# Retention and two MLPs on one core: a batch's last two units in one transfer, whole units further ahead, position factors grown on ScalarE

## The chip, the cores and the metric

The kernel runs on one core of a Trainium2 chip. The metric is the device time of one execution in microseconds, the median over several runs. It is compared with the same time of the changed kernel; lower is better.

## The reference

What is computed is a retention layer (attention without softmax, with a decay in place of it) and two MLPs behind it, all in float32:

```python
scores = scale * np.matmul(q, k.transpose(0, 1, 3, 2))          # 4 batches, 8 heads, 576 positions, 64
gamma = 1.0 - 2.0 ** (-5.0 - np.arange(H))
Dmat = np.where(rel >= 0, gamma[:, None, None] ** rel[None, :, :], 0.0)   # rel = i - j
x = np.matmul(scores * Dmat, v)                                 # as 2304 tokens x 512
h = x @ w_in                                                    # 512 x 2048
x = (h * np.tanh(softplus(h))) @ w_out                          # Mish
h = x @ w2_in
out = (h * sigmoid(1.702 * h)) @ w2_out                         # 2304 x 512
```

## The kernel before

A *unit* is one batch's chunk of 128 positions, all eight heads. A batch has five units; the last holds only 64 positions. So there are 20 units, 0 to 19, and units 4, 9, 14 and 19 are the short ones. The attention loop goes over the units in order. For each unit TensorE multiplies keys and queries (`sc`, line 772), adds to a running sum of keys times values (`ds`, line 795, in PSUM; a copy of it, `state`, is made by ScalarE), and multiplies out (`o`, lines 823 and 834): the state with the queries, then the masked scores `pm` with the values. VectorE makes `pm` from `sc` (line 776) and writes X, which is `o` times position factors `gt` (line 848). GpSimd multiplies the values by the decay (line 761). The scores of unit u + 1 stand on TensorE ahead of unit u's update and outputs.

The position factors `gt` of the first chunk are grown from 16 columns to 128 by doubling, on VectorE (lines 854 and 856); those of the later chunks come from the first by ScalarE. The tables for this ride behind unit 0's data, in the same buffer.

All loads are issued by SP, in the order in which the program writes them, to one DMA queue of 16 engines. A whole unit is one transfer of 1 MB (queries, keys twice, values; rows of 8 KB). A short unit is two transfers, of 128 x 2 KB and 64 x 2 KB. There are five unit buffers, used in turn, and a unit's load is written four units ahead of its use (`UNITS_AHEAD`): a load into a used buffer waits on SP until TensorE and GpSimd are done with the unit that was in it, and everything behind it on SP waits too. The first two weights of the first MLP (`w1[0]`, `w1[1]`, 1 MB each) are fetched between the units at the places that `EARLY_AT` gives; the other weights follow behind the last unit. They are converted in several steps on VectorE, ScalarE and GpSimd in the gaps of the attention loop. Their places in SBUF (`w0` to `w9` of the pool `keep`) are empty until then.

The first MLP's blocks begin on TensorE inside the last three units of the attention loop; behind these come the layers, about 750 us long, in which TensorE is the busy engine.

Of the kernel before, what the change touches and what calls it, by code (L numbers as in the profile page):

```python
# [8 lines left out]
F32 = mybir.dt.float32  # L9
# [5 lines left out]
ALU = mybir.AluOpType  # L15
# [3 lines left out]
B, H, S, D = 4, 8, 576, 64  # L19
NT, DM, DFF = 2304, 512, 2048  # L20
P = 128
NPAIR = H // 2
# [3 lines left out]
CH = [(c, min(P, S - c)) for c in range(0, S, P)]  # L26
NCH = len(CH)
UNITS = [(b, c) for b in range(B) for c in range(NCH)]
# [31 lines left out]

KEPT = 10
X_UNITS = (4, 5, 6, 7, 10, 11, 12, 13)
EARLY_AT = ((1, 5), (7, 13))
EARLY = len(EARLY_AT)
LATE = [-2 + 1.95 * i for i in range(NM - EARLY)]
UNITS_AHEAD = 4
GROW = (16, 32, 64)
TABLES = NCH * H + NPAIR * (NCH + len(GROW) + GROW[0])
FIRST = 4 * DM + (TABLES + 15) // 16 * 16

# [23 lines left out]


@with_exitstack
def retention_mish_gelu_kernel(ctx: ExitStack, tc: tile.TileContext, qkv, w1, w2, first_unit, out):
    nc = tc.nc  # L100
    keep = ctx.enter_context(tc.tile_pool(name="keep", bufs=1))
    dram = ctx.enter_context(tc.tile_pool(name="dram", bufs=1, space=DRAM))
# [16 lines left out]
    def act(o, i, f=AF.Copy, scale=1.0, bias=0.0):  # L119
        nc.scalar.activation(out=o, in_=i, func=f, scale=scale, bias=bias)  # L120
# [18 lines left out]
    def plan(name, step, job):  # L139
        plans.setdefault(name, []).append((step, job))  # L140
        plans[name].sort(key=lambda p: p[0])

    def position(name, step):
        for j in [j for j in under_way if j[1] == name]:
            j[1] = next(j[0], None)
            if j[1] is None:
                under_way.remove(j)
        while plans.get(name) and plans[name][0][0] <= step:
            job = plans[name].pop(0)[1]
            then = next(job, None)  # L150
            if then:
                under_way.append([job, then])
# [8 lines left out]
    def fetch(m):  # L161

        raw = place(m + 1).tile([P, 2 * DM], I64, tag=f"w{m + 1}", name="raw")
        if m < EARLY:
            nc.sync.dma_start(out=raw, in_=w1[m])
        else:
            for i in range(2):
                nc.sync.dma_start(out=raw[:, i * DM : (i + 1) * DM], in_=w1[m][:, i * DM : (i + 1) * DM])
        held[m] = raw.rearrange("p (q n) -> p q n", q=4)
        return  # L170
        yield
# [122 lines left out]
    n_u = len(UNITS)  # L294
# [8 lines left out]

    for m, (loaded_in, converted_in) in enumerate(EARLY_AT):
        plan("fetch", loaded_in - n_u, fetch(m))
# [177 lines left out]
    while not units or sum(units[-1]) < N_ROUND * STEPS:  # L483
        first = sum(units[-1]) if units else 0
# [214 lines left out]
    def attention():  # L699
        with tc.tile_pool(name="att", bufs=1) as ap:  # L700
            loaded = {}

            def load(u):
                if u >= len(UNITS):
                    return
                b, c = UNITS[u]
                n = CH[c][1]
                t = buffers[u % len(buffers)]
                w = NPAIR * n
                if n < P:  # L710
                    pieces = [(P, 0, 2 * w), (n, 2 * w, 2 * w + DM)]
                else:
                    pieces = [(P, 0, 2 * DM), (P, 2 * DM, FIRST)] if u == 0 else [(P, 0, 4 * DM)]
                for rows, e0, e in pieces:
                    nc.sync.dma_start(out=t[:rows, e0:e], in_=first_unit[:, e0:e] if u == 0 else qkv[b, c, :rows, e0:e])
                loaded[u] = (
                    t[:, :w].rearrange("p (c s) -> p c s", c=NPAIR),
                    t[:, w : 2 * w].rearrange("p (c s) -> p c s", c=NPAIR),
                    t[:, 2 * w : 2 * w + DM],
                    t[:, 2 * w + DM : 2 * w + 2 * DM],  # L720
                )

            state = [ap.tile([P, NPAIR, P], F32, name=f"state{i}") for i in range(2)]
            for t in (state[1][:, 0], state[1][:, 1:]):
                nc.gpsimd.memset(t, 0.0)
            nc.vector.memset(state[0], 0.0)
            buffers = [
                ap.tile([P, 4 * DM if i else FIRST], F32, name=f"unit{i}") for i in range(UNITS_AHEAD + 1)
            ]
            tab = buffers[0][:, 4 * DM : 4 * DM + TABLES]  # L730
            vt = tab[:, : NCH * H].rearrange("p (c h) -> p c h", c=NCH)
            per_pair = tab[:, NCH * H :].rearrange("p (c n) -> p c n", c=NPAIR)
            steps, grow, first = (
                per_pair[:, :, :NCH],
                per_pair[:, :, NCH : NCH + len(GROW)],
                per_pair[:, :, NCH + len(GROW) :],
            )
# [4 lines left out]
                out=cm, in_=cm, pattern=[[1, P]], compare_op=ALU.is_ge, fill=0.0, base=0, channel_multiplier=-1  # L742
            )
            gt = ap.tile([P, NCH, NPAIR, P], F32, name="gt")
# [4 lines left out]

            act(column[:, :1], state[0][:, 0, :1], AF.Mish)  # L750

            load(1)
            for u in range(2, UNITS_AHEAD):
                load(u)
            pm, sums, now = {}, [None], [None]

            def decay_v(u):
                b, c = UNITS[u]
                n = CH[c][1]
                vv = loaded[u][2][:n].rearrange("p (h d) -> p h d", d=D)  # L760
                nc.gpsimd.tensor_tensor(  # L761
                    out=vv, in0=vv, in1=vt[:n, c, :].unsqueeze(2).to_broadcast([n, H, D]), op=ALU.mult
                )

            def scores(u):
                n = CH[UNITS[u][1]][1]
                qt, kt = loaded[u][:2]
                sc = [quarters(bank("sc", (0, 1, 2, 3))) for _ in range(2)]
                for p in range(NPAIR):
                    for j in range(2):  # L770
                        sl = slice(64 * j, 64 * j + 64)
                        nc.tensor.matmul(sc[j][:n, p, :n], lhsT=kt[sl, p, :], rhs=qt[sl, p, :], start=True, stop=True)  # L772
                pm[u] = []
                for j in range(2):
                    t = ap.tile([P, NPAIR, P], F32, tag="pm", name="pm", bufs=4)
                    nc.vector.tensor_tensor(  # L776
                        out=t[:n, :, :n],
                        in0=sc[j][:n, :, :n],
                        in1=cm[:n, :n].unsqueeze(1).to_broadcast([n, NPAIR, n]),
                        op=ALU.mult,  # L780
                    )
                    pm[u].append(t)
# [21 lines left out]
            def take(u):  # L804

                if UNITS[u][1] == NCH - 1:
                    return None
                for j in range(2):
                    sl = slice(64 * j, 64 * j + 64)
                    act(state[u % 2][sl, :, sl], sums[0][sl, :, :D])  # L810
                return state[u % 2]
# [39 lines left out]

            scores(0)
            decay_v(0)
            nc.vector.tensor_copy(out=gt[:, 0, :, : GROW[0]], in_=first)
            for j, w in enumerate(GROW):
                nc.vector.tensor_tensor(  # L856
                    out=gt[:, 0, :, w : 2 * w],
                    in0=gt[:, 0, :, :w],
                    in1=grow[:, :, j : j + 1].to_broadcast([P, NPAIR, w]),
                    op=ALU.mult,  # L860
                )
            for u in range(n_u):
                step = u - n_u
                load(u + UNITS_AHEAD)
                if u + 1 < n_u:
                    decay_v(u + 1)
                position("pool", step)
                position("fetch", step)
                if 1 < u < n_u - 1:
                    scores(u + 1)  # L870
                update(u)
                now[0], before = take(u), now[0]
                o = outputs(u, before)
                if u == 1:
                    scores(u + 1)
                if u < NCH - 1:
                    n = CH[u + 1][1]
                    for p in range(NPAIR):
                        act(gt[:, u + 1, p, :n], gt[:, 0, p, :n], scale=steps[:, p, u + 1 : u + 2])
                position("act early", step)  # L880

                if u == n_u - 2:
                    elementwise(0, jobs=False)
                finish(u, o)
                if u == n_u - 1:
                    elementwise(1, jobs=False)
                if u == 0:
                    scores(1)
                position("vector", step)
                position("act late", step)  # L890
                if u in X_UNITS:
                    k = X_UNITS.index(u)
                    split_x((0, SIDE)[k // NK], k % NK)()
                if u == n_u - 3:
                    up(0)
                if u == n_u - 2:
                    up(1)
# [101 lines left out]
```

## Time and profile before

| | |
|---|---|
| median of 3 runs | 819.74 us (818.33 to 820.0) |
| the profiled execution | 818.37 us |
| its span, first to last instruction | 816.6 us |
| TensorE (PE) busy | 810.1 us, 99% |
| VectorE (DVE) busy | 554.2 us, 68% |
| ScalarE (ACT) busy | 405.4 us, 50% |
| GpSimd (POOL) busy | 114.9 us, 14% |
| attention stage | from the start to about 72.7 us |

The span is what the profiler saw of the program; the time of the execution has 1.8 us around it. Busy TensorE is counted from pipelined matmuls, so 99% means that it hardly stood still, not that it ran at its peak. The attention stage is the only one that the change touches.

### The profile page before, as it was taken

How to read it: one execution, taken by the hardware profiler on the slowest of the kernel's cores; microseconds unless marked ns; L12 is line 12 of the kernel's file. 1: busy time of each engine (PE TensorE's matmuls, PEld its weight loads, DVE VectorE, ACT ScalarE, POOL GpSimd, SP SyncE). 2: the span in 40 equal slices, each digit the busy share in tenths (PEclk: the TensorE clock that was granted, in tenths of full speed). 3: DMA queues.
4: the chain of work that ended last, by engine and by line, in shares of the span. 5: the costliest groups of instructions: out<-in, count | busy, mean ns of one | idle time of the engine just before them, and what ended most of it. 6: DMA issues, size and time to landing. Idle time of an engine off the chain costs nothing.

```text
span 816.6 us, 13465 instructions
## 1 busy us (share of the span) xinstructions
PE 810.1 (99%) x5104; PEld 742.1 (91%) x5104; DVE 554.2 (68%) x1030; ACT 405.4 (50%) x748; POOL 114.9 (14%) x124
## 2 busy tenths in 40 slices
PE   9999999999999999999999999999999999999998
PEld 8898888888888888888888899999999999999998
DVE  4886866655876778777645455699655898555776
ACT  4445766664554556455443333566233665233553
POOL 3442322221122214133210000000000000000000
PEclk9999999999999999999999999999999999999999
DMA  9999600002487749578531377787877878877774
GB/s 348 381 342 406 259 1 0 1 10 94 149 243 220 238 128 271 169 233 246 178 102 41 110 272 254 240 275 253 321 254 235 269 271 265 297 255 244 261 266 168
DMA packets 96048, 175.01 MB, mean 214 GB/s; under 512 B 5232, under 2 KB 67184, under 8 KB 90224
## 3 DMA queue, kind: packets, MB, share of 16 engines
q1 hardware_dynamic: 95840, 173.96, 63.3%
q8 instruction: 40, 0.66, 0.3%
q14 instruction: 24, 0.20, 0.1%
q10 hardware_dynamic: 144, 0.20, 0.1%
HBM read 140.06 MB, written 34.08 MB: 213 GB/s over the span
## 4 chain that ended last, share of the span: by engine, by line
PE 96%; DMA 2%; DVE 1%; ACT 0%; POOL 0%; issue 0%; SPq 0%; DVEq 0%
PE h L348 24%; PE acc L369 24%; PE p L592 21%; PE p L637 21%; PE sc L772 2%; PE o L834 2%; DMA unit<-qkv_dram 1%; PE o L823 1%; PE ds L795 1%; DMA unit<-first_unit_dram 1%; DVE pm L776 0%; DVE gt L856 0%; POOL unit L761 0%; DVE X L848 0%; DVE g L398 0%
## 5 line engine op out<-in xcount | busy, mean ns | idle before, releaser
L369 PE MATMUL acc<-g,w 128*128 128x512 f32 (+1 forms) x960 | 209.5, 368 | 0.0
L369 PEld LDWEIGHTS acc<-g,w 128*128 128x128 f32 x960 | 168.4, 189 | 30.4
L348 PE MATMUL h<-x,w 128*128 128x512 f32 x768 | 184.7, 390 | 0.1
L592 PE MATMUL p<-xop,ring 128*128 128x384 f32 x1008 | 175.2, 334 | 0.0
L637 PE MATMUL p<-g,ring 128*128 128x384 f32 x1008 | 175.2, 334 | 0.0
L592 PEld LDWEIGHTS p<-xop,ring 128*128 128x128 f32 x1008 | 174.8, 188 | 0.1
L637 PEld LDWEIGHTS p<-g,ring 128*128 128x128 f32 x1008 | 174.8, 188 | 0.0
L348 PEld LDWEIGHTS h<-x,w 128*128 128x128 f32 x768 | 143.8, 188 | 30.4 <-DVE w L237 0.5
L398 DVE TENSOR_TENSOR g<-c,g 128x512 fp32r<-128x512 f32 x80 | 55.6, 695 | 103.4 <-ACT g L120 103.2
L120 ACT ACTIVATE g<-cs 128x384 fp32r<-128x384 f32 x168 | 87.8, 524 | 63.3 <-PE p L637 62.4
L430 DVE TENSOR_TENSOR g<-cs,g 128x384 fp32r<-128x384 f32 x168 | 92.5, 557 | 26.1 <-ACT g L120 25.0
L120 ACT ACTIVATE g<-c 128x512 fp32r<-128x512 f32 x80 | 47.2, 589 | 113.1 <-PE acc L369 112.4
L120 ACT ACTIVATE cs<-cs 128x384 f32<-128x384 f32 x72 | 37.8, 526 | 111.6 <-DVE cs L430 111.6
L200 POOL TENSOR_TENSOR cy<-cr 128x256 int32<-128x256 int32 x64 | 54.2, 866 | 178.2 <-DVE cr L196 94.5
L120 ACT ACTIVATE c<-h 128x512 f32<-128x512 f32 x80 | 44.2, 552 | 44.8 <-PE h L348 41.4
L430 DVE TENSOR_TENSOR cs<-cs 128x384 f32<-128x384 f32 x96 | 53.1, 553 | 0.8
L200 POOL TENSOR_TENSOR raw<-raw 128x512 int32<-128x512 int32 x30 | 34.7, 1157 | 87.3 <-DVE raw L196 87.3
L120 ACT ACTIVATE cr<-cr 128x512 int32<-128x512 uint32 x68 | 41.4, 663 | 1.3 <-DVE cr L184 1.3
L430 DVE TENSOR_TENSOR u<-p,s 128x384 f32<-128x384 f32 x30 | 16.7, 556 | 34.9 <-PE p L592 34.9
L120 ACT ACTIVATE raw<-raw 128x512 int32<-128x512 uint32 (+1 forms) x60 | 37.5, 673 | 4.9 <-DVE raw L184 4.8
L285 DVE TENSOR_TENSOR cy<-cy,cr 128x896 fp32r<-128x896 f32 x32 | 37.8, 1187 | 2.7 <-ACT cr L120 2.0
L430 DVE TENSOR_TENSOR cs<-p,u 128x384 f32<-128x384 f32 x48 | 26.8, 557 | 11.0 <-PE p L592 10.2
(64 smaller groups left out, 644.2 us busy)
## 6 DMA issues: line engine op xcount, KB each, us to landing
ring<-stream SPq DMA_DIRECT2D x112, 512.0 KB, 4.6
ring<-stream SPq DMA_DIRECT2D x28, 1024.0 KB, 4.8
cr<-w_dram SPq DMA_DIRECT2D x34, 512.0 KB, 4.5
unit<-qkv_dram SPq DMA_DIRECT2D x15, 1024.0 KB, 7.5
stream<-cr SPq DMA_DIRECT2D x32, 448.0 KB, 2.8
stream<-cy SPq DMA_DIRECT2D x32, 448.0 KB, 3.3
raw<-w_dram SPq DMA_DIRECT2D x26, 512.0 KB, 9.9
out_dram<-X SPq DMA_DIRECT2D x11, 192.0 KB, 3.0
```

Source lines behind the costliest of these rows:

```text
L120: nc.scalar.activation(out=o, in_=i, func=f, scale=scale, bias=bias)
L200: nc.gpsimd.tensor_tensor(out=o, in0=upper, in1=bits, op=ALU.add)
L285: nc.vector.tensor_tensor(out=y, in0=v, in1=hi.bitcast(F32), op=ALU.subtract)
L348: nc.tensor.matmul(h[:, :n], lhsT=W[m][:, a, k * P : (k + 1) * P], rhs=xs[t, k][:, b, :n], start=((k, a, b) == order[0]), stop=((k, a, b) ...
L369: nc.tensor.matmul(acc[t, e][:, :n], lhsT=W[m][:, a, DM + e * P : DM + (e + 1) * P], rhs=g[:, b, :n],  start=(begins(i) and a == 0 and b = ...
L398: lambda: nc.vector.tensor_tensor(out=g[:, 1, :n], in0=c[:, :n], in1=g[:, 0, :n].bitcast(F32), op=ALU.subtract),
L430: eng.tensor_tensor(out=o, in0=a, in1=b, op=op)
L592: nc.tensor.matmul(banks[p], lhsT=w[:, a, k * P : (k + 1) * P], rhs=x[:, b, k], start=(p not in SAME and k == 0 and a == 0 and b == 0), st ...
L637: nc.tensor.matmul(banks[e, p], lhsT=w[:, a, e * P : (e + 1) * P], rhs=g[:, b], start=(p != 2 and r == 0 and a == 0 and b == 0), stop=(r = ...
L772: nc.tensor.matmul(sc[j][:n, p, :n], lhsT=kt[sl, p, :], rhs=qt[sl, p, :], start=True, stop=True)
L795: nc.tensor.matmul(sums[0][64 * j : 64 * j + 64, p, :D], lhsT=kk[:, sl], rhs=v[:, sl], start=(c == 0 and p == 0), stop=True, skip_group_ch ...
L834: nc.tensor.matmul(o[sl, p, :n], lhsT=v[:n, p * P + 64 * j : p * P + 64 * j + 64], rhs=pm[u][j][:n, p, :n], start=(c == 0 and p == 0), sto ...
```

## The change

It does four things. The units of a batch that are loaded whole are now its first three (`wide`: units 0, 1, 2, 5, 6, 7, 10, ...); each is a transfer of 1 MB as before. The last two units of a batch, one whole and one short, come in one transfer of 128 rows of 12 KB, 1.5 MB, from a new input `batch_ends` into one buffer, `ends_of`; the host packs it. The whole units get six buffers: three of their own and three lent from the weight places `w7`, `w8` and `w9`. And the growth of `gt` starts from 32 columns, as one copy and eight multiplies on ScalarE, in place of one copy and three multiplies on VectorE. The tables are 64 columns longer for it. The first weight's fetch is written at unit 0 instead of unit 1.

```diff
-EARLY_AT = ((1, 5), (7, 13))
+EARLY_AT = ((0, 5), (7, 13))
...
-UNITS_AHEAD = 4
-GROW = (16, 32, 64)
+LENT = (7, 8, 9)
+OWN = 3
+GROW = (32, 64)
...
+REST = CH[-1][1]
+LAST = 4 * DM + 2 * NPAIR * REST + DM
...
+            def load(u):
+
+                b, c = UNITS[u]
+                if c == NCH - 2:
+                    nc.sync.dma_start(out=ends_of, in_=batch_ends[b])
+                    loaded[u] = views(ends_of, P)
+                    loaded[u + 1] = views(ends_of[:, 4 * DM :], REST)
+                    return
+                t = buffers[(u - b * 2) % len(buffers)]
...
-            buffers = [
-                ap.tile([P, 4 * DM if i else FIRST], F32, name=f"unit{i}") for i in range(UNITS_AHEAD + 1)
-            ]
+            buffers = [ap.tile([P, 4 * DM if i else FIRST], F32, name=f"unit{i}") for i in range(OWN)]
+            buffers += [keep.tile([P, 4 * DM], F32, tag=f"w{i}", name="unit") for i in LENT]
+            ends_of = ap.tile([P, LAST], F32, name="ends_of")
+            wide = [u for u in range(n_u) if UNITS[u][1] < NCH - 2]
...
-            load(1)
-            for u in range(2, UNITS_AHEAD):
-                load(u)
+            for u in range(1, NCH + 1):
+                if u != NCH - 1:
+                    load(u)
...
-            nc.vector.tensor_copy(out=gt[:, 0, :, : GROW[0]], in_=first)
+            act(gt[:, 0, :, : GROW[0]], first)
             for j, w in enumerate(GROW):
-                nc.vector.tensor_tensor(
-                    out=gt[:, 0, :, w : 2 * w],
-                    in0=gt[:, 0, :, :w],
-                    in1=grow[:, :, j : j + 1].to_broadcast([P, NPAIR, w]),
-                    op=ALU.mult,
-                )
+                for p in range(NPAIR):
+                    act(gt[:, 0, p, w : 2 * w], gt[:, 0, p, :w], scale=grow[:, p, j : j + 1])
             for u in range(n_u):
                 step = u - n_u
-                load(u + UNITS_AHEAD)
+                if u and UNITS[u - 1][1] == NCH - 1 and u + NCH - 2 < n_u:
+                    load(u + NCH - 2)
+                if u - 1 in wide and wide.index(u - 1) + len(buffers) < len(wide):
+                    load(wide[wide.index(u - 1) + len(buffers)])
...
+                if u == 0:
+                    for n in wide[NCH - 1 : len(buffers)]:
+                        load(n)
```

On SP, the first places of the program before, from unit 3's load on (`unit_79` is unit 3, `unit_80` unit 4 in two pieces, `unit_76` to `unit_79` behind these units 5 to 8, `raw` the first weight; what a load waits for stands behind it):

```order
L715 DMA unit_79<-qkv_dram 128x2048
L715 DMA unit_80<-qkv_dram 128x512
L715 DMA unit_80<-qkv_dram 64x512
L715 DMA unit_76<-qkv_dram 128x2048 [waits DMAHW0_49,DMAHW1_49,PE_49,Pool_49]
L165 DMA raw<-w_dram 128x1024
L715 DMA unit_77<-qkv_dram 128x2048 [waits DMAHW2_49,PE_49,Pool_49]
L715 DMA unit_78<-qkv_dram 128x2048 [waits DMAHW3_49,PE_49,Pool_49]
L715 DMA unit_79<-qkv_dram 128x2048 [waits DMAHW4_49,PE_49,Pool_49]
L715 DMA unit_80<-qkv_dram 128x512 [waits DMAHW5_49,PE_49]
L715 DMA unit_80<-qkv_dram 64x512 [waits DMAHW6_49,PE_49,Pool_49]
```

The same places of the changed program (the first `ends_of` is units 3 and 4; `unit_79`, `unit_80` and `unit_81` are units 5, 6 and 7 in the lent places; `unit0_76`, `unit1_77` and `unit2_78` are units 10, 11 and 12; the second `ends_of` is units 8 and 9, and the `unit_79` behind it unit 15):

```order
L719 DMA ends_of_82<-batch_ends_dram 128x3072
L728 DMA unit_79<-qkv_dram 128x2048
L168 DMA raw_128<-w1_dram 128x1024
L728 DMA unit_80<-qkv_dram 128x2048
L728 DMA unit_81<-qkv_dram 128x2048 [waits DMAHW0_49]
L728 DMA unit0_76<-qkv_dram 128x2048 [waits DMAHW1_49,PE_49,Pool_49]
L728 DMA unit1_77<-qkv_dram 128x2048 [waits DMAHW2_49,PE_49,Pool_49]
L728 DMA unit2_78<-qkv_dram 128x2048 [waits DMAHW3_49,PE_49,Pool_49]
L719 DMA ends_of_82<-batch_ends_dram 128x3072 [waits DMAHW4_49,PE_49,Pool_49]
L728 DMA unit_79<-qkv_dram 128x2048 [waits DMAHW5_49,PE_49,Pool_49]
```

Units 6 and 7 moved up to the loads that wait for no engine, and units 10 to 12 stand ahead of units 8 and 9.

On TensorE the order of the blocks is the same in both. Before, from unit 6's last state outputs over unit 8's scores to unit 7's update (`unit_77`, `unit_79` and `unit_78` are units 6, 8 and 7):

```order
L823 MATMUL o<-unit_77,state_72 64x128 x7
L834 MATMUL o<-pm,unit_77 64x128 [waits DVE_49] x2
L834 MATMUL o<-pm,unit_77 64x128 x6
L772 MATMUL sc<-unit_79 128x128 [waits DMAHW3_49,PE_49]
L772 MATMUL sc<-unit_79 128x128 [waits PE_49]
L772 MATMUL sc<-unit_79 128x128 x6
L795 MATMUL ds<-unit_78 64x64 [waits Activation_49,Pool_49]
```

The same place of the changed program (`unit` is a lent place, so unit 6 or 7; `ends_of` holds unit 8):

```order
L832 MATMUL o<-unit,state_72 64x128 x7
L843 MATMUL o<-pm,unit 64x128 [waits DVE_49] x2
L843 MATMUL o<-pm,unit 64x128 x6
L781 MATMUL sc<-ends_of 128x128 [waits DMAHW4_49,PE_49]
L781 MATMUL sc<-ends_of 128x128 [waits PE_49]
L781 MATMUL sc<-ends_of 128x128 x6
L804 MATMUL ds<-unit 64x64 [waits Activation_49,Pool_49]
```

Unit 8's scores took their data from a whole-unit buffer and now take it from `ends_of`, for whose transfer they wait; unit 7's update and outputs stand behind them.

On VectorE, the first rows of before (`pm` of unit 0, the growth of `gt`, X of unit 0, then `pm` of units 1 and 2):

```order
L776 TENSOR_TENSOR pm<-sc,cm 128x512 [waits PE_49]
L854 COPY gt<-unit_76 128x4x16 [waits DMAHW1_49]
L856 TENSOR_TENSOR gt<-gt,unit_76 128x4x16 [waits DVE_49]
L856 TENSOR_TENSOR gt<-gt,unit_76 128x4x32 [waits DVE_49]
L856 TENSOR_TENSOR gt<-gt,unit_76 128x4x64 [waits DVE_49]
L848 TENSOR_TENSOR X<-o,gt 128x4x128 [waits DVE_49,PE_49]
L776 TENSOR_TENSOR pm<-sc,cm 128x512 [waits PE_49] x4
```

On ScalarE, the first rows of the changed program (growth, unit 0's state, then the second chunk's factors):

```order
L123 ACTIVATE gt<-unit_76 128x4x32 [waits DMAHW1_49]
L123 ACTIVATE gt<-gt,unit_76 128x32 [waits Activation_49]
L123 ACTIVATE gt<-gt,unit_76 128x32 x3
L123 ACTIVATE gt<-gt,unit_76 128x64 [waits Activation_49] x4
L123 ACTIVATE state_71<-ds 64x4x64 [waits PE_49]
L123 ACTIVATE state_71<-ds 64x4x64
L123 ACTIVATE gt<-gt,unit_76 128x128 [waits Activation_49] x4
```

The four growth rows left VectorE, where X of unit 0 now stands right behind `pm` of unit 0, and stand ahead of unit 0's state on ScalarE.

## Rows read from the trace of the kernel before

**Rows 1.** The page: busy us, share and instructions; GB/s in 40 slices of the span.

```profile
PE 810.1 (99%) x5104; PEld 742.1 (91%) x5104; DVE 554.2 (68%) x1030; ACT 405.4 (50%) x748; POOL 114.9 (14%) x124
...
GB/s 348 381 342 406 259 1 0 1 10 94 149 243 220 238 128 271 169 233 246 178 102 41 110 272 254 240 275 253 321 254 235 269 271 265 297 255 244 261 266 168
```

**Rows 2.** Waits of TensorE, 8 to 70 us: total us, times, longest.

```profile
PE sc L772 <- DMA unit<-qkv_dram: 1.5, 1, 1.5
```

**Rows 3.** The chain that ended last: start us, us, what.

```profile
13.47 10.91 DMA unit<-qkv_dram
```

**Rows 4.** Timeline of TensorE, 0 to 33 us: start, us, group [idle before].

```profile
1.05 3.79 PE L748 MATMUL unused<-state 128*128 128x128 f32 x16 [1.05 <-POOL state L725]
4.77 2.08 PE L772 MATMUL sc<-unit 64*128 64x128 f32 x16
...
9.32 1.16 PE L772 MATMUL sc<-unit 64*128 64x128 f32 x16
...
11.80 1.60 PE L834 MATMUL o<-pm,unit 128*64 128x128 f32 x16
13.33 2.06 PE L772 MATMUL sc<-unit 64*128 64x128 f32 x32
...
22.36 0.68 PE L834 MATMUL o<-pm,unit 64*64 64x64 f32 x16
24.52 1.16 PE L772 MATMUL sc<-unit 64*128 64x128 f32 x16 [1.48 <-DMA unit<-qkv_dram]
...
30.56 1.16 PE L772 MATMUL sc<-unit 64*128 64x128 f32 x16
```

**Rows 5.** Timeline of TensorE, 33 to 65 us: scores of units 11, 13, 16, 18.

```profile
39.31 1.16 PE L772 MATMUL sc<-unit 64*128 64x128 f32 x16
...
45.56 1.16 PE L772 MATMUL sc<-unit 64*128 64x128 f32 x16
...
54.31 1.16 PE L772 MATMUL sc<-unit 64*128 64x128 f32 x16
...
60.35 1.16 PE L772 MATMUL sc<-unit 64*128 64x128 f32 x16
```

**Rows 6.** Timeline of SP: issues of unit 0's first piece, the weight, units 7 and 18.

```profile
0.80 0.38 SPq L715 DMA_DIRECT2D unit<-first_unit_dram  x1
...
9.84 0.43 SPq L165 DMA_DIRECT2D raw<-w_dram  x1
...
17.83 0.33 SPq L715 DMA_DIRECT2D unit<-qkv_dram  x1
...
52.15 0.33 SPq L715 DMA_DIRECT2D unit<-qkv_dram  x1
```

**Rows 7.** DMA issues of the same four moments: KB each, us from issue to landing.

```profile
unit<-first_unit_dram SPq DMA_DIRECT2D x1, 512.0 KB, 3.6
...
raw<-w_dram SPq DMA_DIRECT2D x1, 1024.0 KB, 11.5
...
unit<-qkv_dram SPq DMA_DIRECT2D x1, 1024.0 KB, 9.0
...
unit<-qkv_dram SPq DMA_DIRECT2D x1, 1024.0 KB, 6.0
```

**Rows 8.** Windows: length, PE, PEld, DVE, ACT, POOL busy, PEclk, DMA share, GB/s.

```profile
13.00:14.00 1.00, 1.00 (x18) 0.83 (x16) 0.00 (x0) 0.68 (x3) 0.67 (x1) 1.00 0.88 127
...
70.00:80.00 10.00, 10.00 (x82) 8.70 (x82) 7.88 (x15) 7.27 (x14) 2.30 (x2) 1.00 1.03 416
```

**Rows 9.** Timeline of VectorE: growth of the factors, pm of unit 1.

```profile
8.38 1.88 DVE L856 TENSOR_TENSOR gt<-gt,unit 128x64 f32<-128x64 f32 x3
...
10.98 1.28 DVE L776 TENSOR_TENSOR pm<-sc,cm 128x512 f32<-128x512 f32 x2
```

**Rows 10.** Timeline of ScalarE: position factors of 128 and of 64 columns.

```profile
12.41 1.28 ACT L120 ACTIVATE gt<-gt,unit 128x128 f32<-128x128 f32 x4
...
19.89 1.06 ACT L120 ACTIVATE gt<-gt,unit 128x64 f32<-128x64 f32 x4
```

## What the change is forecast to do

> **What bounds the kernel now.** I began with the busy shares: TensorE is busy 810 of 816.6 us [rows 1], so time can be won or lost only where TensorE stands still, or where something makes it stand still that does not now. The list of TensorE's waits says where that is after the start: its one wait of note, 1.5 us, is for a unit's transfer [rows 2]. The chain gives the place of the first: the transfer issued at 13.47 took 10.91 us to land, and the scores of unit 6 began right behind it, at 24.52 [rows 3, 4]. From there TensorE's rows follow without a gap through the attention stage, so each later score block starts when the block ahead of it is done, with its data already there.
>
> What makes the data just about early enough is the DMA queue. Its sixteen engines are full from the start: 348, 381, 342 and 406 GB/s in the first four slices of 20.4 us [rows 1]. A transfer of 1 MB needs 2.5 us at the 416 GB/s of an undisturbed stretch [rows 8]; that these take 9 to 11 us from issue to landing means that they stand behind others. Three in a row show in which order: the first weight was issued at 9.84 and took 11.5, so it landed at 21.3; unit 6 was issued at 13.47 and landed at 24.4; unit 7 was issued at 17.83, took 9.0 and landed at 26.8 [rows 3, 6, 7]. They land in the order of their issue, 3.1 and 2.4 us apart. So a transfer's landing is the sum of all bytes issued ahead of it, and the order in which SP issues them is the first thing to read in the change.
>
> **The change part by part.** *Order of the loads.* Call e0 to e3 the new 1.5 MB transfers of a batch's units 3 and 4. There is one buffer for them, so e1 can be issued only when unit 4's outputs are done on TensorE, while the six whole-unit places let units 10, 11 and 12, of the third batch, be issued as soon as units 0, 1 and 2 are done. SP's rows show the outcome: u10, u11 and u12 stand ahead of e1, although TensorE wants e1 (the scores of unit 8) first and u10 two units later. Before, SP's order was the order of use.
>
> What must have landed before unit 8's scores can start, after the first 512 KB: 616 + 1024 + 1024 + 1536 (e0) + 1024 (u5) + 1024 (weight) + 5 x 1024 (u6, u7, u10, u11, u12) + 1536 (e1) = 12904 KB, or 13.21 MB. That first piece is issued at 0.80 and lands 3.6 us later, at 4.4 [rows 6, 7]. At 416 GB/s [rows 8] the 13.21 MB need 31.8 us and end at 36.2. Before, from 4.4 to unit 7's landing at 26.8, there were 584 + 3 x 1024 + 384 + 4 x 1024 = 8136 KB, 8.33 MB in 22.4 us, or 372 GB/s; at this rate e1 lands at 39.9. A part of that slowness lies at the two narrow pieces of unit 4, which the change takes away: while they were moved the engines were 0.88 busy and moved 127 GB/s [rows 8]. I take 405 GB/s, nearer to the clean stretch: 32.6 us, landing at 37.0. Unit 8's scores then start at 37.1 and not at 30.56 [rows 4]: **+6.5 us** (5.7 to 9.4). Whether SP issues e1 a little earlier does not matter, since it stands behind the bytes of 29 us.
>
> TensorE would have been there long before. Its own way to unit 8: the growth of the position factors leaves VectorE (three multiplies, 1.88 us, [rows 9]), so pm of unit 1, which started at 10.98 behind them, can start as soon as unit 1's scores are done, at 10.5, and the outputs that took 1.60 instead of some 1.04 us [rows 4] get shorter: 0.6 us won. On ScalarE the growth is one copy and eight multiplies. Four of 128 columns took 1.28 us, four of 64 took 1.06 [rows 10]; 64 columns less save 0.22, so four of 32 come to some 0.95 and the whole to 0.33 + 0.95 + 1.06 = 2.3 us, from the second piece's landing (616 KB behind 4.4, so 5.9) to 8.3, hidden under unit 0's outputs, behind which unit 1's scores begin at 9.32 [rows 4]; the state copy queued behind it is wanted only after those. If it were late, unit 0's X and then pm of unit 1 would be late next. Then e0: it ends 4200 KB behind 4.4, at 14.7, so unit 3's scores start at 14.8 instead of 14.4 (the second half of the 2.06 us from 13.33) [rows 4]. The 0.6 is lost again there and 0.4 more. Unit 5, the weight and unit 6 end at 22.3 and unit 7 at 24.8, so TensorE, which comes to unit 6 at 22.36 + 0.68 + 0.4 = 23.4, does not wait where it waited 1.48 us. From unit 6 to unit 8 it has 6.04 us to go (24.52 to 30.56) [rows 4]. It comes to unit 8 at 29.5 and waits until 37.1, some 7.6 us. Behind unit 8's pm on VectorE and its state on ScalarE stand the conversions of the first weight; that weight is wanted only in the attention's last units, so nothing else waits.
>
> After this TensorE has no idle time in which to catch up [rows 1, 2], so the delay stays to the end.
>
> *The clock after the wait.* At the start TensorE works at the lower of its two levels (1.2 and 2.4 GHz), as its rows show: unit 0's sixteen score records took 2.08 us, the same sixteen of unit 1 took 1.16 [rows 4]. It had been idle before 1.05, and those sixteen end at 6.85, so some 5.8 us ran at half speed and 2.9 us were lost. After the wait of 1.48 us the rows behind it are of full length [rows 4], so a wait of that size costs nothing more. 7.6 us lies beyond it, nearer to the idle state at the start. The cost lies between 0 and 2.9; I take **+2.5 us**, somewhat under the start's, because there the stream of matmuls was itself broken by waits.
>
> The Trainium skill's page "TensorE: Matmul & The Clock Gate", in its section on the HAM clock gate, says that the clock falls to half when the engine has been idle for long and comes back only after sustained work. By it the sum takes this term nearly whole; by the 1.48 us row alone it would take nothing. No row of this trace has a wait long enough to say.
>
> *The later transfers e2 and e3.* Each is issued when the unit before it in the single buffer is done: e2 behind unit 9 (39.31), e3 behind unit 14 (54.31). Their scores follow 6.25 and 6.04 us later (45.56, 60.35) [rows 5]. By then the queue is short. From an empty queue 512 KB took 3.6 us; 1024 KB more at 416 GB/s make 6.1. By the slower row, 1 MB issued at 52.15 that took 6.0 [rows 6, 7], it is 7.3. So e2 costs between 0 and 1.0 and e3 between 0.1 and 1.3; I take 0.4 and 0.5: **+0.9 us**. The raw weights behind e3 land later by about as much, under units 15 to 17.
>
> *At nothing:* fewer issues (19 instead of 27 in the stage; SP only waits there), the first weight's fetch one unit earlier (it stands behind u5 in both), 64 more columns of tables (32 KB, under 0.1 us), the lent places (the weights that live there are fetched after units 15 to 17, behind e3).
>
> Sum: 6.5 + 2.5 + 0.9 = 9.9 on the profiled 818.37 us (span 816.6 and 1.8 around it): 828.3. The median of the runs, 819.74, lies 1.4 above the profiled one; I forecast **829.0** for the changed kernel.
>
> **Rivals.**
> - *The clock stays up.* The wait for e1 comes, but the rows behind it are of normal length. Then 6.5 + 0.9: 818.4 to 819.7 + 7.4 = **826.5**. For it: the wait of 1.48 us left no mark. Against it: the start.
> - *e1 does not wait behind u10 to u12* (not slower). If the engines served transfers of one queue side by side, e1, issued at 23.4, could land 6.1 to 6.6 us later, at 29.5 to 30.0, when TensorE comes for it at 29.5. Unit 8's scores would then start 0.5 to 1.0 before 30.56, and with e2 and e3 the sum would be about 0: **819**. It decides if e1 lands before some 32. Against it: the order of landing in [rows 3, 6, 7] and that transfers side by side would share the 416 GB/s [rows 8].
> - *The fresh 1.5 MB transfers are worse than I think*, and the queue runs at 372 GB/s: 9.4 + 2.9 + 2.3 = 14.6, **833 to 834**. For it: the slow rates before. Against it: their narrow pieces are gone.
>
> **How the numbers follow.** My case 0.60, the clock staying up 0.25, not waiting 0.08, the worse one 0.07. The first two, with their bounds of the rate and of e2 and e3, reach from 824 (5.7 with nothing more, on 818.4) to 833; that is the range, and it leaves out the 0.08 and most of the 0.07. Differences under 0.2% (1.6 us) are about what a measurement of this kernel cannot tell from no change. Only the second rival can end there or on the fast side: same 0.05, faster 0.04 (if e1 lands early and e2 and e3 cost nothing), slower 0.91.
>
> **What the changed profile would show.** Right: one wait of TensorE of 6 to 10 us for the batch_ends transfer, ending at about 37, and this transfer landing behind u12; score blocks of about 2 us right behind the wait; two small waits, 6 us behind units 9 and 14; no wait at unit 6, and VectorE's pm of unit 1 at 10.5. Wrong: unit 8's scores before 32 with TensorE's rows closed ahead of them. Then the queue is not first in, first out, or carries more than the 416 GB/s that I allow.

## The result, and the profile after

The changed kernel takes 828.57 us (median of 5 runs, 827.53 to 828.87) against 819.74 us; the ratio is 1.011, with a 95% interval of 1.0095 to 1.0125. Forecast was 829.0 us in 824 to 833, slower with a chance of 0.91. The profiled execution took 828.80 us, with a span of 827.1, so 10.5 more than before.

The page's busy line and its GB/s line, as in [rows 1]:

```profile
PE 810.4 (98%) x5104; PEld 743.0 (90%) x5104; DVE 549.4 (66%) x1026; ACT 407.9 (49%) x757; POOL 111.3 (13%) x124
...
GB/s 377 425 147 327 418 44 2 1 1 78 118 230 236 192 152 242 207 209 241 202 90 96 101 226 235 267 255 261 298 274 245 260 268 270 299 248 257 257 260 172
```

TensorE's busy time has hardly moved (810.1 before), but that is two things that cancel: at a lower clock, below, it is busy 2.24 us longer, and up to unit 2's scores about as much shorter than before. The queue moves more in the first two slices (377 and 425 GB/s against 348 and 381); then comes a slice of 147 in which it has little to do, and the last 1.5 MB transfer and the weights behind it fill the fourth and fifth. The list of TensorE's waits (total us, times, longest) says for what it stands, where [rows 2] had 1.5 us for a unit:

```profile
PE sc L781 <- DMA ends_of<-batch_ends_dram: 10.7, 4, 6.1
```

The chain (start us, us, what) shows the four transfers, from issue to landing; that of [rows 3] is gone from it:

```profile
2.70 13.12 DMA ends_of<-batch_ends_dram
...
24.85 11.93 DMA ends_of<-batch_ends_dram
...
48.06 6.70 DMA ends_of<-batch_ends_dram
...
63.80 6.87 DMA ends_of<-batch_ends_dram
```

TensorE's timeline (start, us, group [idle before]) shows where they end. The scores from `ends_of` below are those of units 3, 8, 9, 13, 14 and 18; the rows at 22.38 and 24.70 are units 5 and 6.

```profile
15.95 1.16 PE L781 MATMUL sc<-ends_of 64*128 64x128 f32 x16 [2.70 <-DMA ends_of<-batch_ends_dram]
...
22.38 1.16 PE L781 MATMUL sc<-unit 64*128 64x128 f32 x16
...
24.70 1.16 PE L781 MATMUL sc<-unit 64*128 64x128 f32 x16
...
29.77 1.04 PE L843 MATMUL o<-pm,unit 128*64 128x128 f32 x16
36.92 2.08 PE L781 MATMUL sc<-ends_of 64*128 64x128 f32 x16 [6.11 <-DMA ends_of<-batch_ends_dram]
38.93 1.12 PE L804 MATMUL ds<-unit 128*64 128x64 f32 x16
39.83 1.92 PE L832 MATMUL o<-unit,state 128*64 128x128 f32 x16
...
42.61 0.68 PE L781 MATMUL sc<-ends_of 64*64 64x64 f32 x16
...
54.90 1.16 PE L781 MATMUL sc<-ends_of 64*128 64x128 f32 x16 [0.89 <-DMA ends_of<-batch_ends_dram]
58.35 0.68 PE L781 MATMUL sc<-ends_of 64*64 64x64 f32 x16
...
70.81 1.16 PE L781 MATMUL sc<-ends_of 64*128 64x128 f32 x16 [1.05 <-DMA ends_of<-batch_ends_dram]
```

Follow the delay along the starts that [rows 4, 5] give for before. Unit 8's scores: 36.92 - 30.56 = 6.36. Unit 13's: 54.90 - 45.56 = 9.34. Unit 18's: 70.81 - 60.35 = 10.46, and that is the whole difference of the spans. Between units 8 and 9 TensorE does the same work as between 13 and 14, but takes 5.69 us (36.92 to 42.61) instead of 3.45 (54.90 to 58.35). The windows (length, PE, PEld, DVE, ACT, POOL busy, PEclk, DMA share, GB/s) say why:

```profile
34.00:35.00 1.00, 0.00 (x0) 0.00 (x0) 0.00 (x0) 0.00 (x0) 0.00 (x0) 0.95 1.04 438
35.00:36.00 1.00, 0.00 (x0) 0.00 (x0) 0.00 (x0) 0.00 (x0) 0.00 (x0) 0.50 0.96 406
...
40.00:41.00 1.00, 1.00 (x14) 1.00 (x12) 0.28 (x1) 0.80 (x3) 0.00 (x0) 0.50 1.02 434
41.00:42.00 1.00, 1.00 (x16) 1.00 (x14) 0.00 (x0) 1.00 (x2) 0.00 (x0) 0.63 0.95 393
42.00:43.00 1.00, 1.00 (x26) 0.83 (x22) 0.27 (x1) 1.00 (x3) 0.00 (x0) 1.00 0.22 90
```

Some four microseconds into the wait the granted clock falls to 0.50, the lower of the two levels, and rises again between 41 and 42 us, behind some five microseconds of matmuls. So 10.46 = 6.36 (the wait for e1, and 0.25 by which TensorE comes later) + 2.24 (the clock) + 0.74 and 1.12 (e2 and e3).

### The profile page after: what moved, and what is told of

Read it like the earlier page. It is cut to its first block, busy times and chain, and to the rows that moved or that the text cites. A ratio compares the mean times of both kernels' runs of the same rounds, so it can differ in the third digit from the quotient of the medians.

```text
span 827.1 us, 13447 instructions
## 1 busy us (share of the span) xinstructions
PE 810.4 (98%) x5104; PEld 743.0 (90%) x5104; DVE 549.4 (66%) x1026; ACT 407.9 (49%) x757; POOL 111.3 (13%) x124
## 4 chain that ended last, share of the span: by engine, by line
PE 94%; DMA 5%; DVE 0%; ACT 0%; SPq 0%; issue 0%
PE h L351 24%; PE acc L372 24%; PE p L595 21%; PE p L640 21%; DMA ends_of<-batch_ends_dram 5%; PE sc L781 1%; PE o L832 1%; PE o L843 1%; PE ds L804 1%; SPq L728 0%; SPq L726 0%; DVE g L401 0%; ACT w L123 0%; ACT g L123 0%; DVE w L240 0%
## 5 line engine op out<-in xcount | busy, mean ns | idle before, releaser
L203 POOL TENSOR_TENSOR cy<-cr 128x256 int32<-128x256 int32 x64 | 52.5, 842 | 179.8 <-DVE cr L199 97.0
L785 DVE TENSOR_TENSOR pm<-sc,cm 128x512 f32<-128x512 f32 (+1 forms) x40 | 23.5, 627 | 18.7 <-PE sc L781 18.7
```

The lines of the kernel that those rows point to most:

```text
L203: nc.gpsimd.tensor_tensor(out=o, in0=upper, in1=bits, op=ALU.add)
L785: nc.vector.tensor_tensor(out=t[:n, :, :n], in0=sc[j][:n, :, :n], in1=cm[:n, :n].unsqueeze(1).to_broadcast([n, NPAIR, n]), op=ALU.mult,)
```

## The experiments

My theory: (a) e1 is late because the loads of units 10 to 12, needed later, stand ahead of it in one queue; (b) the wait then costs clock; (c) the single buffer makes every ends transfer start too late. Rivals: the 1.5 MB transfers are slow by themselves; the growth on ScalarE or the lent buffers cost time; the 6.1 us are only the queue's rate and would come back under any order. The kernel before was timed again beside each group: 818.44 us (20 runs) beside the first four kernels, 818.42 (21 runs) beside the others.

**Loads of units 10 to 12 moved behind e1.** Written ahead of the `if` that loads whole units:

```diff
                     load(u + NCH - 2)
+                    for n in wide[len(buffers) : 9] if u == NCH else ():
+                        load(n)
-                if u - 1 in wide and wide.index(u - 1) + len(buffers) < len(wide):
+                if u > NCH and u - 1 in wide and wide.index(u - 1) + len(buffers) < len(wide):
```

> The changed kernel with one edit: the loads of units 10, 11 and 12 are written behind e1, the transfer of units 8 and 9, and not ahead of it. Buffers, sizes and everything else stay. My theory (e1 waits behind 3 MB that are wanted later): e1 is issued at 24.9 as before, stands only behind unit 7 (landing at 25.7) and lands at about 31, when TensorE comes for it at 30.8; the wait of 6.1 us shrinks to under 0.7, the clock does not fall (2.35 us), the waits for e2 and e3 (0.9 and 1.05 us) stay: 828.6 - 5.6 - 2.35 = 820.6. Rival (the single buffer and the size of 1.5 MB make the wait, whatever the order): e1 cannot be issued earlier, so it lands as late as before: 827 to 828.6.

Measured: 831.18 us (829.5 to 833.12, 4 runs), ratio 1.0143 (1.0126 to 1.016). The number missed by 10 us. TensorE's timeline, scores of units 3, 8, 13 and 14:

```profile
16.05 2.08 PE L781 MATMUL sc<-ends_of 64*128 64x128 f32 x16 [2.75 <-DMA ends_of<-batch_ends_dram]
...
34.86 1.16 PE L781 MATMUL sc<-ends_of 64*128 64x128 f32 x16 [1.15 <-DMA ends_of<-batch_ends_dram]
...
56.61 2.08 PE L781 MATMUL sc<-ends_of 64*128 64x128 f32 x16 [6.89 <-DMA ends_of<-batch_ends_dram]
63.05 0.68 PE L781 MATMUL sc<-ends_of 64*64 64x64 f32 x16
```

And its chain: e1 and e2, from issue to landing.

```profile
27.75 6.97 DMA ends_of<-batch_ends_dram
...
43.76 12.71 DMA ends_of<-batch_ends_dram
```

The wait at unit 8 shrank from 6.11 to 1.15 us, as (a) says. It came back one batch later at its old size: I had moved units 10 to 12 only, so units 15, 16 and 17 and the second weight (landed at 45.5, 47.9, 52.8 and 50.4) now stood ahead of e2, which landed at 56.47. Two stretches at the lower clock, behind the waits at units 3 and 13, did the rest in the profiled execution, which at 833.12 us is the slowest of the four. That is (a) again, shown at another place, and my oversight in the number.

**The strict order of use, still one buffer.** Units 10 to 12 behind e1, 15 to 17 behind e2:

```diff
                     load(u + NCH - 2)
-                if u - 1 in wide and wide.index(u - 1) + len(buffers) < len(wide):
-                    load(wide[wide.index(u - 1) + len(buffers)])
+                    for n in range(u + NCH, u + NCH + 3):
+                        if n in wide:
+                            load(n)
```

> The changed kernel with its single buffer for the 1.5 MB transfers, and every later load written in the order of use: e1, units 10 to 12, the second weight, e2, units 15 to 17, e3. In the first reordered kernel the wait left unit 8 (6.1 to 1.15 us) and came back at unit 13 (0.9 to 6.9 us), where e2 landed behind units 15, 16, 17 and the second weight. My theory (a transfer lands behind all bytes issued ahead of it, so the long wait sits wherever a 1.5 MB transfer stands behind whole units that are wanted later): now no transfer does; three waits of about 1 us each remain, since each of e1, e2, e3 is issued only when its buffer is free and takes 6.5 to 7 us, and the clock falls at most at unit 3: 821 to 823, 822. Rival (with one buffer the time is lost somewhere, in whatever order): 827 or more.

Measured: 822.79 us (822.63 to 824.7, 4 runs), ratio 1.0055 (1.0041 to 1.007). Its waits and its chain:

```profile
PE sc L781 <- DMA ends_of<-batch_ends_dram: 6.0, 4, 2.7
```

```profile
27.80 7.11 DMA ends_of<-batch_ends_dram
...
43.94 7.18 DMA ends_of<-batch_ends_dram
...
60.16 6.45 DMA ends_of<-batch_ends_dram
```

The profiled execution is the slowest of the four (824.7 us; the others lie within 0.3); 2.7 of the 6.0 us are unit 3's wait, as in the changed kernel. The order alone was worth about 5 us: 5.8 by the medians (828.57 - 822.79), 4.5 by the two ratios to the kernel before. What stays is the single buffer: each ends transfer starts on a nearly empty queue only when the last one's buffer is free, takes about 7 us, and is waited for (1.29, 1.36 and 0.62 us).

**Two ends buffers.** The second is paid for by one more lent place; all loads stand in the order of use, and e1 is issued at unit 0 (the last line):

```diff
-LENT = (7, 8, 9)
-OWN = 3
+LENT = (6, 7, 8, 9)
+OWN = 2
...
+                    ends_of = ends_two[b % 2]
...
-            ends_of = ap.tile([P, LAST], F32, name="ends_of")
+            ends_two = [ap.tile([P, LAST], F32, name=f"ends_of{i}") for i in range(2)]
...
-                if u and UNITS[u - 1][1] == NCH - 1 and u + NCH - 2 < n_u:
-                    load(u + NCH - 2)
+                if u and UNITS[u - 1][1] == NCH - 1 and u + 2 * NCH - 2 < n_u:
+                    load(u + 2 * NCH - 2)
...
+                    load(2 * NCH - 2)
```

> Two buffers for the 1.5 MB transfers (paid for by lending one more weight place), and every load in the order of its use, so that e1 is issued at the start behind unit 7 and e2 and e3 a whole batch earlier. My theory: the waits for e1, e2 and e3 and the low clock all go; only the wait of 2.7 us at unit 3 stays, against the 1.5 us that the kernel before waits at unit 6: unit 8's scores at 30.8 against 30.56, so 819.74 + 0.2 = 820 (no measurable change against the kernel before). Rival (larger rows and earlier loads are worth something of their own once the order is right): 818 or less. Rival (the lent places or the 1.5 MB transfers cost something elsewhere): 822 or more.

Measured: 819.96 us (818.07 to 820.84, 12 runs), ratio 1.0005 (0.9995 to 1.0015). One wait for the transfers is left, at unit 3:

```profile
PE sc L782 <- DMA ends_of<-batch_ends_dram: 2.5, 1, 2.5
```

So, within the interval of 0.2%, neither the size of the transfers, nor the lent places, nor the growth costs the 9 us; they lay in order and buffer.

**The same, and e0 in two transfers** (unit 3's 1 MB first; e1 to e3 stay whole):

```diff
-                    nc.sync.dma_start(out=ends_of, in_=batch_ends[b])
+                    for e0, e in ((0, 4 * DM), (4 * DM, LAST)) if b == 0 else ((0, LAST),):
+                        nc.sync.dma_start(out=ends_of[:, e0:e], in_=batch_ends[b][:, e0:e])
```

> As the kernel with two buffers, and the first batch's e0 issued in two transfers, unit 3's 1 MB and then unit 4's 512 KB. My theory: unit 3 lands at about 13.3 as in the kernel before, and not at 15.8, so the wait of 2.7 us falls to 0.2; TensorE then comes to unit 6 at 22.3, before it has landed (23.1), and waits about 1 us there and some at unit 7: unit 8's scores at about 29.7 against 30.56, 819.74 - 0.9 = 818.8. Rival (the queue as a whole sets unit 8's time, e1 landing at 29.4 and later): 819.7, no gain from the split.

Measured: 817.22 us (817.0 to 818.36, 8 runs), ratio 0.9977 (0.9967 to 0.9987). In TensorE's timeline unit 3 now waits 0.28 us, and unit 6 1.28, with the granted clock up behind both:

```profile
14.31 1.16 PE L783 MATMUL sc<-ends_of 64*128 64x128 f32 x16 [0.28 <-DMA ends_of<-batch_ends_dram]
...
24.41 1.16 PE L783 MATMUL sc<-unit 64*128 64x128 f32 x16 [1.28 <-DMA unit<-qkv_dram]
```

**And the first weight's fetch behind unit 7 and e1**, the same kernel with one more line:

```diff
-EARLY_AT = ((0, 5), (7, 13))
+EARLY_AT = ((1, 8), (7, 13))
```

> The kernel with two buffers and unit 3 in a transfer of its own, and the first weight fetched behind unit 10 and not between units 5 and 6 (its conversion written three units later). My theory (the wait of 1.3 us at unit 6 is the 1 MB of the weight ahead of it): unit 6 lands 2.4 us earlier, the wait goes, unit 8's scores start at 29.3 and not at 30.5: 817.2 - 1.2 = 816.0, a ratio of about 0.9965 to the kernel before. Rival (the conversion, three units later, is late for the first block of the MLP or holds up pm on VectorE): 817.2 or more, with a new wait at the MLP's first block.

Measured: 815.79 us (815.66 to 816.07, 5 runs), ratio 0.9965 (0.9951 to 0.9978): faster than both kernels, with its slowest run below all 41 runs of the kernel before that were taken beside the experiments (817.85 and more). Unit 6 landed at 20.88, e1 at 26.98, the weight at 31.94. The whole list of TensorE's waits names no transfer:

```profile
PE unused L759 <- POOL state L735: 1.1, 1, 1.1
PE ds L806 <- POOL unit L772: 0.5, 1, 0.5
```

The 1 MB of a weight that is wanted only in the attention's last units had stood ahead of units 6 and 7.

**TensorE kept busy during the wait.** The changed kernel with 24 matmuls into unit 8's score banks ahead of its scores; they compute nothing that is used:

```diff
+                for i in range(24 if u == 2 * NCH - 2 else 0):
+                    nc.tensor.matmul(sc[0][:, i % NPAIR, :], lhsT=cm, rhs=cm, start=True, stop=True)
```

> The changed kernel with 24 matmuls of no use (128 columns, of the mask with itself) ahead of unit 8's scores, into the bank that these scores overwrite: about 5.3 us of work for TensorE inside its wait of 6.1 us. If the slow blocks behind the wait come from TensorE's clock, which fell while the engine stood idle, the granted clock stays 1.00, unit 8's scores take 1.16 us and not 2.08, and the time falls by 2.35 to 826.2. If they are slow for another reason (operands just landed, the port shared with the queue), they stay slow: 828.6. Nothing of the reference's result changes.

Measured: 829.99 us (829.3 to 830.71, 4 runs), ratio 1.0128 (1.0115 to 1.0141). TensorE's timeline, the scores of units 3, 8, 9 and 18:

```profile
15.93 1.63 PE L783 MATMUL sc<-ends_of 64*128 64x128 f32 x16 [2.14 <-DMA ends_of<-batch_ends_dram]
...
32.30 5.62 PE L779 MATMUL sc<-cm 128*128 128x128 f32 x48
37.86 1.16 PE L783 MATMUL sc<-ends_of 64*128 64x128 f32 x16
...
41.31 0.68 PE L783 MATMUL sc<-ends_of 64*64 64x64 f32 x16
...
70.41 1.51 PE L783 MATMUL sc<-ends_of 64*128 64x128 f32 x16 [2.04 <-DMA ends_of<-batch_ends_dram]
```

The reading (b) held: without the idle time unit 8 to unit 9 took 3.45 us, not 5.69, and the mean granted clock from 24 to 44 us was 1.00. Nor was it the transfers beside the matmuls, as windows over the same block of work in three runs show (columns as above; from unit 8's to unit 9's scores in the changed kernel and in this one, from unit 13's to unit 14's in the run with units 10 to 12 behind e1):

```profile
36.92:42.61 5.69, 5.69 (x65) 5.29 (x65) 1.29 (x2) 2.40 (x5) 3.03 (x3) 0.58 0.91 384
...
37.86:41.31 3.45, 3.45 (x65) 3.16 (x64) 1.29 (x2) 1.52 (x4) 2.09 (x3) 1.00 0.99 413
...
56.61:63.05 6.44, 6.44 (x64) 5.91 (x64) 1.29 (x2) 1.17 (x3) 4.04 (x4) 0.51 0.01 3
```

With the queue full (413 GB/s) and the clock up the block takes 3.45 us; with the queue empty (3 GB/s) and the clock at 0.51 it takes 6.44.

The expected time did not hold. In this run the clock fell behind the waits of 2.14 and 2.04 us at units 3 and 18, where it had stayed up after 2.70 and 1.05. The first fall made TensorE come to the added matmuls at 32.30 and not at 30.81, so these ran 0.94 us past the scores' former start (37.86 against 36.92), which left 1.3 us of gain at unit 9 (41.31 against 42.61). Of that, e3 took back 1.0: issued at 62.41 and not at 63.80, it took 7.86 us, so that unit 18 started only 0.4 earlier. The second fall took the rest and more. That is the profiled execution; another of the four took 829.3 us at a mean granted clock of 1.0, so the clock does not explain the time of every run.

**The growth alone,** in the kernel before (`GROW = (32, 64)`, the copy and the eight multiplies on ScalarE):

> The kernel before with the growth of the position factors alone taken over: 32 columns from the table, one copy and eight multiplies on ScalarE, none on VectorE. My theory: pm of unit 1 starts about 0.5 us earlier and TensorE is 0.6 us ahead until unit 6, for whose transfer it waits anyway; that wait grows from 1.5 to about 2.1 us and the time is the same: 819 (a ratio of 1.000, within 0.001), unless the longer wait lets the clock fall more often (up to 1.002). Rival (the growth is worth its 0.6 us): a ratio of 0.9993 and a wait of 1.5 us.

Measured: 819.69 us (818.27 to 821.17, 11 runs), ratio 1.0007 (0.9998 to 1.0017). It does what it says and brings nothing here: unit 2's scores start at 12.87 instead of 13.33, and TensorE waits the longer for unit 6:

```profile
24.35 2.08 PE L772 MATMUL sc<-unit 64*128 64x128 f32 x16 [1.76 <-DMA unit<-qkv_dram]
```

**The short unit as one transfer of 128 rows of 4 KB,** in the kernel before:

```diff
-                    pieces = [(P, 0, 2 * w), (n, 2 * w, 2 * w + DM)]
+                    pieces = [(P, 0, 2 * w + DM)]
```

> The kernel before with each short unit in one transfer of 128 rows of 4 KB (512 KB) in place of 128 x 2 KB and 64 x 2 KB (384 KB). My theory (the 2 KB rows slow the queue, 127 GB/s at 13 to 14 us): unit 4 lands at about 14.7 instead of 16.7 though it is 128 KB longer, unit 6 at 23 to 23.5 instead of 24.4, the wait at unit 6 shrinks from 1.5 to under 0.7 us and the clock falls less often: ratio 0.998 to 0.999. Rival (the queue was slow there for another reason): unit 6 lands 0.3 us later and the ratio is 1.000 or above.

Measured: 819.49 us (817.69 to 819.86, 11 runs), ratio 1.0005 (0.9996 to 1.0014). Missed. The windows show the repair, at the place of [rows 8] (127 GB/s there):

```profile
13.00:14.00 1.00, 0.74 (x14) 0.63 (x12) 0.82 (x2) 0.00 (x0) 0.66 (x1) 1.00 0.99 250
```

Unit 6 landed at 23.71 and not at 24.4. But TensorE came to it at 22.22 and not at 23.04, since unit 0's sixteen score records took 1.16 us in this execution and not 2.08, waited 1.63 us, and the granted clock fell to 0.50 behind that:

```profile
23.85 1.61 PE L772 MATMUL sc<-unit 64*128 64x128 f32 x16 [1.63 <-DMA unit<-qkv_dram]
```

Whether the 0.7 us of the queue are worth anything on average, this interval does not tell.

## Why the prediction was right

*The queue is first in, first out, and carries what is ahead.* Right, and it is the core of the result: units 10, 11 and 12 landed at 28.1, 30.6 and 33.1, e1 at 36.78 (forecast 37.0). The two experiments on the order show the cause by moving it. *The size, +6.5:* 6.36 measured. The rate was right too: the 13.21 MB from 4.4 to 36.78 us are 408 GB/s, where I took 405. (The window from 30 to 40 us has 427; a landing is that of the last of the 16 engines, and the first had ended e1 at 34.88.) TensorE came to unit 8 at 30.81, not at 29.5, so the wait itself was 6.11 us instead of 7.6; the landing set the start of the scores, so this did not touch the sum.

*TensorE's own way to unit 8* is what I mis-sized, by 1.3 us (30.81 for 29.5). I let e0 land at 14.7; it landed at 15.82, and unit 3's scores waited 2.70 us (15.95, forecast 14.8). I had taken a sum of bytes at one rate from unit 0's landing. Its engines ended e0 one after another, the first at 14.0 and the last at 15.8, and a landing is that of the last. That the wait of 1.48 us at unit 6 goes was right: the row at 24.70 has no idle time ahead of it. The growth too: on ScalarE the copy starts at 5.90 and the eight multiplies, 1.91 us in all, end at 8.15 (forecast 5.9 and 8.3), and VectorE's `pm` of unit 1 starts at 9.73 instead of 10.98. That is 0.8 before my 10.5; unit 1's scores stood 0.78 earlier here (8.54 against 9.32), mainly because unit 0's took 1.16 us and not 2.08.

*The clock, +2.5:* 2.24. The keep-busy experiment shows it to be the clock and nothing of the transfer. The Trainium skill's page "TensorE: Matmul & The Clock Gate", section on the HAM clock gate, has this fall after a long idle time and return after sustained work; the trace agrees for the 6.11 us. Two readings of mine were weaker than I took them. The bound of 2.9 came from the start, which I put at the lower level by the length of unit 0's records. They are as long (2.08 us) as those behind the wait for e1, but the granted clock of the kernel before reads 1.00 there, so the trace does not show the start's level by itself:

```profile
5.00:6.00 1.00, 1.00 (x11) 1.00 (x12) 0.00 (x0) 0.00 (x0) 0.13 (x1) 1.00 1.08 453
```

And from the row at 24.52 [rows 4] I read that "a wait of that size costs nothing more". One execution was too little for that: behind 1.63 us the clock fell in another run (last section).

*e2 and e3, +0.9:* the mechanism was right, the sizes low: 0.74 and 1.12, together 1.9. From issue to landing the fresh 1.5 MB took 6.70 and 6.87 us where I had 6.1 from a clean rate, with 7.3 as the bound.

*The rivals.* "The clock stays up" fell with the 0.50 in the windows; "e1 does not wait behind u10 to u12" with the order of landing; "worse transfers" with the 408 GB/s, though its price for e2 and e3, 2.3, was nearer to the 1.9 measured than my 0.9. Of the change's four parts the one with the promise, wide rows and buffers ahead, is sound: with a second ends buffer, the order of use, e0 split and the weight behind, it gives 815.79 us. Before, the order of use came by itself, since every load waited for one ring of five buffers; six free buffers for one kind and one for the other broke it.

*The total.* On the profiled executions the 9.9 of the sum stand against 10.43 us (818.37 to 828.80), on the medians against 8.83, because the 819.74 of the kernel before came from the slower of two groups of times (last section). The 829.0 was set between the two bases, and that it lies within 0.5 of the median is in part luck.

## What to carry to other kernels

When one queue serves several kinds of buffers, the kind with the most free places runs ahead and the kind with one place lands last, whatever is wanted first. So write out what is issued in which order, add up the bytes ahead of each transfer, and compare its landing with the moment when the slowest engine wants it; a deeper prefetch of what is wanted later is a cost. And fix an order for all batches at once: mending it in one only handed the same wait to the next.

## What the runs showed of the hardware

The kernel before has two groups of times. Of its 41 runs beside the experiments 22 lie between 817.85 and 818.46 us, with a mean granted clock of 0.999 or 1.0, and 19 between 819.4 and 820.5, all but one at 0.997 or 0.998; none lies between (of its five runs beside the result one does, at 818.86). The profiled execution was of the first group, and its median of three, 819.74, came from the second. Profiled runs with waits between 1.6 and 2.8 us at units 3, 6 or 18 show what the second group may be: the granted clock fell to 0.50 behind waits of 1.63, 1.76, 2.04, 2.14, 2.49, 2.71 and 2.75 us, and stayed up behind others of 1.48 and 2.70. Two microseconds of waiting thus cost 1.5 to 2.8 more in some executions and nothing in others, and these runs do not show what decides it; the kernel whose list of waits names no transfer had all five runs within 0.41 us. That the wait at unit 6 is what parts the two groups of the kernel before was not tried by itself.

The start varies as well: the sixteen score records of unit 0 took 1.16, 1.58, 1.82 or 2.08 us in profiles of kernels that are the same up to there. The granted clock reads 1.00 there in all ten profiles, so what varies is not shown. The difference moved the next blocks by up to 0.8 us, and so decided how long the next transfer was waited for.
